# Narrower products with the low part of v, one copy on GpSimd moved, and a fixed order that ends one product later

## The chip, the cores and the metric

The kernel runs on one core of a Trainium2 chip. A core has engines with instruction streams of their own: TensorE (PE, matrix products; PEld is its loading of the stationary operand), VectorE (DVE), ScalarE (ACT), GpSimd (POOL) and SyncE (SP, which here issues the transfers between the chip's memory and the core's SBUF). Products land in PSUM and are read from there by VectorE and ScalarE. The engines run beside each other and meet through semaphores only. The metric is the device time of one execution in microseconds (us), the median of several runs.

## What is computed

One transformer block on x (2048 rows of 576): a modulated layer norm, linear attention with 32 heads of 18 columns, and a feed-forward network of 4608 hidden columns. Cut to what matters here:

```python
def reference(A_x, A_wqkv, A_wo, B_x, B_w1, B_w2, c, w_mod):
    ...
    h = _layernorm(x, axis=-1) * (1 + ca) + sa
    ...
    pq, pk = phi(q), phi(k)
    kv = jnp.einsum("bhsd,bhse->bhde", pk, v)
    z = jnp.einsum("bhsd->bhd", pk)
    num = jnp.einsum("bhqd,bhde->bhqe", pq, kv)
    den = jnp.einsum("bhqd,bhd->bhq", pq, z)[..., None] + 1e-6
    o = num / den
    ...
    x = x + ga * _A_ref(h, A_wqkv, A_wo)
    h = _layernorm(x, axis=-1) * (1 + cb) + sb
    x = x + gb * _B_ref(h, B_w1, B_w2)
    return x
```

The state sums of the title are kv and z: sums over all 2048 rows of products of pk and v.

## The kernel before

**Numbers in two parts.** TensorE works here on rounded 32-bit data (float32r). Each operand a is split into a high part, a rounded, and a low part, a minus that, rounded again; a product is then the sum of high x high, high x low and low x high. The state sums have a fourth term: pk holds its two parts side by side (`pk[t % 2]`, 128 rows x 2 x 632), and one product with the high part of v moves 128 columns of each of them, 256 in all; the product with the low part of v does the same, so low x low is summed too. v lies in five groups of seven heads (`NHC`, 126 columns, `HG`), with a column of ones that gives z.

**Stages.** The rows are worked in 16 tiles t of 128, four to a block of 512. The first stage (to about 208 us) normalises, projects to k, v and q, and sums the state: `kv_mm(t - 1)` (L581) is called once for each tile, with ten products into the three PSUM tiles kvp. The second stage (to about 370 us) takes, for each tile, pn = phi(q) / den (`q_norm`, L742), transposes it and multiplies it with the joined matrix M; the first feed-forward units run between. `attn_step` (L1192) issues, for a tile s, `prod` = phi(q) * z on GpSimd (L1195), then den and its reciprocal r on VectorE and ScalarE (L748 to L751), then on GpSimd pn = phi(q) * r (L752) and a copy of pn's last 64 columns to its padding (L754):

```python
G.tensor_mul(pn[:, :D].rearrange("p (h d) -> p h d", d=DH), a.rearrange("p (h d) -> p h d", d=DH),
             r.unsqueeze(2).to_broadcast([P, H, DH]))
G.tensor_copy(pn[:, D:], pn[:, KC * P : D])
```

`q_transpose` (L808) turns pn in five blocks of 128 columns; the fifth is columns 512 to 639 and so reads the padding. The third stage, 370 us to the end, is the main part of the feed-forward network: 17 groups of 256 hidden columns, each for two halves of the rows, 34 units in all. A unit has seven `up` products (L1323, six or eight instructions each) and 14 `down` groups (L1396, six instructions each, named ha, hb, hc, hd, he after their left operand), which run one unit later, between the next unit's up products. In the order `DOWN` the second half of a unit ends with he (m = 13), which is summed onto a PSUM bank that an hc group (m = 11) had used and VectorE had read. There are two down tiles in rotation; VectorE adds each group from PSUM to `acc` or `U` (L1404), and the next group into that bank waits for it.

**What sets the order.** A scheduler places instructions that no order is written for. For most of the program up to the end of the second unit of the main part, the order on each engine is written out: `ORDERS` is a table of places, engine by engine, and `arrange()` (L100) gives each instruction in it a dependence, without a wait, on the one ahead of it. The numbers count an engine's instructions in the order in which they were issued in the code. From the third unit on, a manual schedule over all engines holds the order of the code. `arrange()` is called between the two, when only the instructions of the first part have been made: TensorE's table ends at 2585, the last of them.

Of the kernel before, what the change touches and what calls it, by code (L numbers as in the profile page):

```python
# [16 lines left out]
P = 128  # L17
# [5 lines left out]
def kernel(ctx: ExitStack, tc, A_x, A_wqkv, A_wo, B_x, B_w1, B_w2, c, w_mod, out):  # L23
# [20 lines left out]
    HG = 7 * DH  # L44
# [7 lines left out]
    def f32(ap):  # L52
# [1 line left out]

    ORDERS = {
        "PE": """
            0-105 114 106-108 115 109-113 116-2585
        """,
        "DVE": """
            2-3 1 0 4 6-7 11-12 8 5 13-14 18 15 9 16 10 17 19-24 29 25 28 26-27 30-31 43-44 33-34 36-37 35 38 32 39  # L60
# [31 lines left out]
            382-383 386 388 390-395 397 396  # L92
        """,
        "Pool": """
            3 6 0 4-5 2 7 9 8 10-15 20 16-17 19 18 21-26 34 28 27 31 29-30 35 32 38 36 42 33 37 45 39-40 48 43-44 51
            46 41 47 55 49-50 58 52-53 61 85 56 73 57 54 59 77 60 62-63 80 64 74 65 68 75 69 78 66 72 70 79 67 76 81
            71 82-84 95 90-93 86-88 94 101 89 103 105 99-100 97 106-107 121 98 96 102 123 104 108-111 124 114 125
            113 112 115 118 116 119-120 117 122 126-128
# [8 lines left out]
    def arrange():  # L107
        for engine, text in ORDERS.items():
            traced = [i for i in nc.cur_bb.bb.instructions if i.engine == getattr(mybir.EngineType, engine)
                      and not isinstance(i, (mybir.BassTilePoolBoundary, mybir.InstTileManualSchedule))]  # L110
            before = None
            for part in text.split():
                first, *last = part.split("-")
                for i in traced[int(first) : int(last[0] if last else first) + 1]:
                    if before is not None:
                        no_wait = mybir.DependencyInfo(mybir.DependencyClass.NoSync, mybir.DependencyReason.DATA)
                        tc.add_manual_dep(i, before.name, no_wait, reason="arrange")
                    before = i
# [185 lines left out]
    def mod_ps(k):  # L304
        return kvp[k // 2][:, k % 2, :]
# [276 lines left out]
    def kv_mm(t):  # L582

        pkt, vt = pk[t % 2], vx[t % 2]
        for j in range(NHC):
            o = mod_ps(j)
            for h in range(2):
                T.matmul(  # L588
                    o, vt[:, j, h, :], pkt[:, :, j * HG : j * HG + P],
                    start=(t == 0 and h == 0 and j % 2 == 0), stop=(t == NT - 1 and h == 1),  # L590
                    skip_group_check=True,
                )
# [47 lines left out]
    with tc.manual_schedule(engines={mybir.EngineType.PE}):  # L640
        for t in range(NT):
# [35 lines left out]
            if t > 0:  # L677
                kv_mm(t - 1)
            for _ in range((0, 2, 1, 1)[t] if t < 4 else 1):
                q = next(qs)  # L680
# [9 lines left out]
    with tc.manual_schedule(engines={mybir.EngineType.PE}):  # L690
        qs = iter(range(QB, NT))
        finish_wo()
        edges_of_wo(range(NHC - 2))
        q_proj(next(qs))
        kv_mm(NT - 1)
        edges_of_wo((NHC - 2,))

# [20 lines left out]
        for j, kv in enumerate(kvp):  # L718
            n = min(2, NHC - 2 * j)
# [48 lines left out]
        for j in range(KC + 1):  # L768
            psm = ps2()
            n = wo_rows[j]  # L770
# [302 lines left out]
    def fetch(i):  # L1073
        if i < len(streamed):
            _, q, n = streamed[i]
            in_room[i] = parts = []
            left = hd[q, n].shape[1]
            for room, m in rooms0.get(i) or [(rooms[(i + 2) % 3], left)]:
                nc.sync.dma_start(f32(room[:, :m, :]), hd[q, n][:, len(parts) : len(parts) + m, :])
                parts += [room[:, a, :] for a in range(m)]  # L1080
# [427 lines left out]
    def run(tokens, units, weights):  # L1508
        for token in tokens:
            name = token.rstrip("'^")  # L1510
            if name == "ft":
                i = next(fetches)
                if i > 6:
                    fetch(i)
                continue
            late = len(token) - len(name)
            of = weights[late] if name[0] in "wgl" else units[late]
            if of:
                of.step(name)
# [3 lines left out]
    def do_unit(g, p):  # L1523
        nonlocal unit, before, behind2
        unit = Unit(g, p, ws[g])
        for q, lines in enumerate(steps(p)):
            def beside(tokens):
                run(tokens, (unit, before, behind2), (ws[g], ws.get(g + 1)))

            if unit.last and p == 1:  # L1530
                lines = [x + LAST.get((q, j), "").split() for j, x in enumerate(lines)]
            if before:
                before.down(2 * q)
            beside(lines[0])
            unit.up(ORDER[q])
            if not before and q == 1:
                rooms.append(rs.tile([P, 5, 512], F32R, name="room"))
                fetch(6)
            beside(lines[1])
            if before:  # L1540
                before.down(2 * q + 1)
            beside(lines[2])
        behind2, before = before, unit
# [3 lines left out]
    with tc.manual_schedule(engines={mybir.EngineType.PE}):  # L1547
# [3 lines left out]
        ws.update({g: Weights(g) for g in range(2, NG)})  # L1551
        for u in units[:2]:
            do_unit(*u)
    arrange()
    with tc.manual_schedule(engines=ENGINES):
        for u in units[2:]:
            do_unit(*u)
        for work, tokens in TAIL:
            unit.plain_down(work)
            run(tokens.split(), (unit, behind2), ())  # L1560
    psC.release()
    for p in (rs, ph, pf, pu, w2p, wqp, edge, wp, hTa, accp):
        p.release()
# [28 lines left out]
```

## Time and profile before

| | |
|---|---|
| median of 3 runs | 1142.06 us (1140.82 to 1143.03) |
| the profiled execution | 1139.88 us |
| its span, first to last instruction | 1138.1 us |
| granted TensorE clock, mean | 1.00 |
| ACT busy, share of the span | 47% |
| POOL busy, share of the span | 57% |
| mean transfer rate | 236 GB/s |

The profile is of one execution; the 1.8 us between its time and its span lie before the first and after the last instruction. A row of the timeline gives the start in us, the time to the end of the last of a group of equal instructions, the engine, the line of the kernel, the operation, what is written and read, the shape and the count; in brackets stands how long the engine stood idle before it and what ended that. PE's products overlap: the distance between two starts is what one costs, and a duration is longer than that. In the table by stretches a row gives, for a stretch of time, the busy time and count of PE, PEld, DVE, ACT and POOL, then the granted clock, the busy share of the transfer engines and GB/s.

### The profile page before, as it was taken

Reading aid. Unit: us, or ns where it says so; the run is one execution under the profiler, and the core shown is the slowest. Engines: PE = TensorE matmul, PEld = TensorE weight load, DVE = VectorE, ACT = ScalarE, POOL = GpSimd, SP = SyncE. Lnnn points to the kernel's source line nnn. Section 1 sums busy time; section 2 is a strip of 40 time slices with the busy share of each in tenths; the row PEclk is TensorE's granted clock in tenths of the full one; section 3 lists DMA queues with packets and bytes.
Section 4 is the critical chain, followed back from the end, with each engine's and each line's share of the span. In section 5 each row is a group of like instructions: output and inputs, shape, how many; then the busy total and the mean of one; then the engine's idle time right before and its main releaser. Section 6 shows DMA issues by size and latency. Waiting matters only on the chain.

```text
span 1138.1 us, 19287 instructions
## 1 busy us (share of the span) xinstructions
PE 1126.6 (99%) x7033; PEld 1041.0 (91%) x7033; DVE 970.6 (85%) x1543; ACT 538.8 (47%) x1112; POOL 649.4 (57%) x743
## 2 busy tenths in 40 slices
PE   8999999999999999999999999999999999999998
PEld 8999999999998889999999999999999999999998
DVE  7866743685879889999999999999999999999996
ACT  6643442547556544445444444454454444444441
POOL 2100000373715767766775777677767767776776
PEclk9999999999999999999999999999999999999999
DMA  9521100223359976977968779769678697697684
GB/s 281 198 84 33 42 7 1 71 84 115 141 194 340 350 262 252 359 270 267 346 262 330 300 257 350 273 255 363 265 284 332 265 342 285 256 344 275 258 306 156
DMA packets 58813, 269.03 MB, mean 236 GB/s; under 512 B 5724, under 2 KB 21856, under 8 KB 35680
## 3 DMA queue, kind: packets, MB, share of 16 engines
q1 hardware_dynamic: 58708, 267.80, 63.8%
q8 instruction: 56, 0.92, 0.3%
q14 instruction: 37, 0.30, 0.1%
q10 hardware_dynamic: 12, 0.00, 0.0%
HBM read 250.12 MB, written 16.78 MB: 235 GB/s over the span
## 4 chain that ended last, share of the span: by engine, by line
PE 93%; DVE 2%; DMA 1%; POOL 1%; ACT 1%; issue 0%; DVEq 0%; POOLq 0%
PE up L1323 34%; PE down L1396 32%; PE psK L226 12%; PE big L226 6%; PE big L896 2%; PE small L885 2%; PE kvp L588 2%; PE small L214 1%; DMA hT<-hd 1%; PE big L811 1%; PE psT L214 1%; PE kvp L412 1%; DMA raw<-in_w_mod_dram 1%; PE up L1426 1%; PE down L1426 1%; POOL prod L1195 0%
## 5 line engine op out<-in xcount | busy, mean ns | idle before, releaser
L1404 DVE TENSOR_TENSOR acc<-down,acc 128x576 f32<-128x576 f32 x330 | 246.2, 753 | 14.6 <-PE down L1396 5.3
L1323 PE MATMUL up<-hT,w 128*128 128x512 f32 x916 | 239.4, 390 | 0.1
L1323 PEld LDWEIGHTS up<-hT,w 128*128 128x128 f32 x916 | 164.5, 188 | 25.0 <-DMA hT<-hd 0.3
L1358 POOL TENSOR_TENSOR s<-f,f 128x256 f32<-128x256 f32 x66 | 51.6, 782 | 162.0 <-ACT f L1339 162.0
L1396 PE MATMUL down<-w,hb 128*128 128x288 f32 x792 | 120.6, 294 | 0.0
L1396 PE MATMUL down<-w,hc 128*128 128x288 f32 x792 | 120.6, 294 | 0.0
L1396 PEld LDWEIGHTS down<-w,hb 128*128 128x128 f32 x792 | 113.8, 188 | 5.1
L1396 PEld LDWEIGHTS down<-w,hc 128*128 128x128 f32 x792 | 113.7, 188 | 5.1
L121 DVE TENSOR_TENSOR w<-v,w 128x288 fp32r<-128x288 f32 (+1 forms) x170 | 114.4, 682 | 0.5 <-ACT w L1057 0.5
L1404 DVE TENSOR_TENSOR U<-down,U 128x576 f32<-128x576 f32 x132 | 99.5, 754 | 17.5 <-PE down L1396 15.6
L226 PE MATMUL psK<-w,hT 128*128 128x352 f32 (+3 forms) x506 | 106.2, 336 | 0.5 <-POOL w L317 0.5
L1323 PE MATMUL up<-room,w 128*128 128x512 f32 x348 | 91.0, 390 | 0.0
L1377 POOL TENSOR_TENSOR hc<-s,hc 128x512 fp32r<-128x512 f32 x66 | 89.4, 1354 | 0.0
L226 PEld LDWEIGHTS psK<-w,hT 128*128 128x128 f32 x506 | 82.0, 189 | 6.8 <-POOL w L317 0.7
L1339 ACT ACTIVATE f<-f 128x512 f32<-128x512 f32 x102 | 64.4, 631 | 48.9 <-DVE f L1344 26.5
L184 POOL TENSOR_TENSOR rstd<-ve,neghalf 128x4 f32<-128x4 f32 (+3 forms) x10 | 9.8, 977 | 134.5 <-DVE ve L183 134.4
L1342 DVE TENSOR_TENSOR f<-up,p 128x512 f32<-128x512 f32 x102 | 69.6, 683 | 12.8 <-PE up L1323 11.9
L1065 ACT CAST w<-v 128x288 fp32r<-128x288 f32 x85 | 36.7, 434 | 75.4 <-PE down L1396 65.9
L1362 POOL TENSOR_TENSOR f<-f,s 128x256 f32<-128x256 f32 x66 | 50.7, 769 | 36.3 <-DVE hb L1377 25.9
L1323 PEld LDWEIGHTS up<-room,w 128*128 128x128 f32 x348 | 62.5, 188 | 9.4
L1396 PE MATMUL down<-w,hd 128*128 128x288 f32 x396 | 63.0, 294 | 0.9 <-DVE acc L1404 0.9
L1396 PE MATMUL down<-w,ha 128*128 128x288 f32 x396 | 63.0, 294 | 0.0
(310 smaller groups left out, 2529.4 us busy)
## 6 DMA issues: line engine op xcount, KB each, us to landing
hT<-hd SPq DMA_DIRECT2D x66, 1280.0 KB, 5.9
hT<-hd SPq DMA_DIRECT2D x45, 1024.0 KB, 5.3
room<-hd SPq DMA_DIRECT2D x35, 1280.0 KB, 5.6
room<-hd SPq DMA_DIRECT2D x20, 1024.0 KB, 5.3
v<-in_B_w_dram SPq DMA_DIRECT2D x17, 576.0 KB, 6.7
v<-in_B_w_dram SPq DMA_DIRECT2D x17, 512.0 KB, 7.0
hd<-S SPq DMA_DIRECT2D x6, 1024.0 KB, 4.3
xt<-in_A_x_dram SPq DMA_DIRECT2D x16, 288.0 KB, 3.1
```

Source lines behind the costliest of these rows:

```text
L121: return V.tensor_sub(lo, full, f32(hi))
L214: T.transpose(ps[:, i * P : (i + 1) * P], xt[i][:, cidx * P : (cidx + 1) * P], ident)
L226: T.matmul(ps, xpart(a), wpart(b), start=n == 0, stop=n == len(XW) - 1)
L1065: A.copy(self.w2[n][:, 0], src)
L1323: T.matmul(ps, left, right, start=first and m == 0, stop=m == len(seq) - 1, skip_group_check=True)
L1339: A.activation(self.f[i, k], self.f[i, k], AF.Silu)
L1342: V.tensor_add(f, self.bank[bank[1]], self.p1)
L1358: G.tensor_add(self.s[:, 0:1], half(i, 0, 1), half(i, 1, 1))
L1362: G.tensor_sub(half(i, 1, 0), half(i, 1, 0), self.s[:, 1:2])
L1377: eng.tensor_sub(t[:, :, 1, :], src, f32(t[:, :, 0, :]))
L1396: T.matmul(ps[:, p, :HALF], self.a[i, n][:, u, p * P : (p + 1) * P], self.w.w2[n][:, v], start=n in (1, 5, 7, 6) and j == 0, stop=j == 2, ...
L1404: V.tensor_add(dst, ps[:, :, :HALF], dst)
```

## The change

```diff
     ORDERS = {
         "PE": """
-            0-105 114 106-108 115 109-113 116-2585
+            0-105 114 106-108 115 109-113 116-2586
         """,
...
         "Pool": """
-            3 6 0 4-5 2 7 9 8 10-15 20 16-17 19 18 21-26 34 28 27 31 29-30 35 32 38 36 42 33 37 45 39-40 48 43-44 51
+            3 6 0 4-5 2 7 9 8 10-15 20 16-17 19 18 21-26 34 28 27 31 29-30 35 32 38 36 33 42 37 45 39-40 48 43-44 51
...
         for j in range(NHC):
-            o = mod_ps(j)
+            o = mod_ps(j).rearrange("p (a q) -> p a q", a=2)
             for h in range(2):
+                n = 2 - h
                 T.matmul(
-                    o, vt[:, j, h, :], pkt[:, :, j * HG : j * HG + P],
+                    o[:, :n], vt[:, j, h, :], pkt[:, :n, j * HG : j * HG + P],
                     start=(t == 0 and h == 0 and j % 2 == 0), stop=(t == NT - 1 and h == 1),
...
             do_unit(*u)
-    arrange()
     with tc.manual_schedule(engines=ENGINES):
         for u in units[2:]:
             do_unit(*u)
         for work, tokens in TAIL:
             unit.plain_down(work)
             run(tokens.split(), (unit, behind2), ())
+    arrange()
```

Three things. The product with the low part of v (h = 1) takes the high part of pk alone, so low x low is no longer summed; as many products are issued. On GpSimd the copy to pn's padding with the number 33 stands ahead of a product with the number 42, and no longer behind it. And TensorE's table takes in product 2586, the first of the third unit; since that is made later, `arrange()` is called at the end.

On TensorE in the first stage, kv_mm for one tile (kvp are the PSUM tiles of the state sums, pk and vx the parts of pk and v) before:

```order
L588 MATMUL kvp_108<-pk_150,vx_152 128x256 x4
L588 MATMUL kvp_109<-pk_150,vx_152 128x256 x4
L588 MATMUL kvp_110<-pk_150,vx_152 128x256 x2
L226 MATMUL psK<-wq,hT 128x288 x56
L226 MATMUL psK<-w,hT 128x352
```

and now:

```order
L589 MATMUL kvp_108<-pk_150,vx_152 128x128
L589 MATMUL kvp_109<-pk_150,vx_152 128x256
L589 MATMUL kvp_109<-pk_150,vx_152 128x128
L589 MATMUL kvp_109<-pk_150,vx_152 128x256
L589 MATMUL kvp_109<-pk_150,vx_152 128x128
L589 MATMUL kvp_110<-pk_150,vx_152 128x256
L589 MATMUL kvp_110<-pk_150,vx_152 128x128
L226 MATMUL psK<-wq,hT 128x288 x56
```

Every second product has 128 columns; what stands around them is the same.

On GpSimd in the second stage, from the product for tile 5 on (pn_2453 is the pn of tile 3, pn_2524 that of tile 4; acc holds phi(q)), before:

```order
L1195 TENSOR_TENSOR prod_2610<-acc1_96,z_94 128x576
L752 TENSOR_TENSOR pn_2524<-acc1_96,r_2528 128x576
L1195 TENSOR_TENSOR prod_2676<-acc1_96,z_94 128x576
L754 COPY pn_2453<-pn_2453 128x64
L754 COPY pn_2524<-pn_2524 128x64
L1195 TENSOR_TENSOR prod_2768<-acc1_96,z_94 128x576
```

and now:

```order
L1196 TENSOR_TENSOR prod_2610<-acc1_96,z_94 128x576
L753 TENSOR_TENSOR pn_2524<-acc1_96,r_2528 128x576
L755 COPY pn_2453<-pn_2453 128x64
L1196 TENSOR_TENSOR prod_2676<-acc1_96,z_94 128x576
L755 COPY pn_2524<-pn_2524 128x64
L1196 TENSOR_TENSOR prod_2768<-acc1_96,z_94 128x576
```

The copy for the earlier pn is one product further ahead; the other stays behind that product.

On TensorE in the third stage, where the second unit ends and the third begins (he_4371 is the second unit's last down group, ha_4366 and hd_4387 the first two that belong to the third unit's order), before:

```order
L1396 MATMUL down<-w_4244,hc_4326 128x288 x6
L1323 MATMUL up<-hT,w 128x512 x6
L1323 MATMUL up<-hT,wtb 128x512 x2
L1396 MATMUL down<-w_4197,ha_4366 128x288 x6
L1323 MATMUL up<-hT,w 128x512 x6
L1396 MATMUL down<-w_4264,he_4371 128x288 x6
L1396 MATMUL down<-w_4206,hd_4387 128x288 x6
```

and now:

```order
L1397 MATMUL down<-w_4244,hc_4326 128x288 x6
L1324 MATMUL up<-hT,w 128x512 x6
L1324 MATMUL up<-hT,wtb 128x512 x2
L1397 MATMUL down<-w_4264,he_4371 128x288 x6
L1397 MATMUL down<-w_4197,ha_4366 128x288 x6
L1324 MATMUL up<-hT,w 128x512 x6
L1397 MATMUL down<-w_4206,hd_4387 128x288 x6
```

he stands two groups further ahead, and between it and hd there are now ha and an up product. The other engines' orders are as before, and so is that of the transfers.

## The prediction

> **What bounds the kernel now.** I read the page first: busy times and the chain of waits.
>
> ```profile
> span 1138.1 us, 19287 instructions
> ...
> PE 1126.6 (99%) x7033; PEld 1041.0 (91%) x7033; DVE 970.6 (85%) x1543; ACT 538.8 (47%) x1112; POOL 649.4 (57%) x743
> ...
> PE 93%; DVE 2%; DMA 1%; POOL 1%; ACT 1%; issue 0%; DVEq 0%; POOLq 0%
> ```
>
> The second row is busy time by engine, the third the share of the chain that ended last. TensorE (PE) works or waits for its own predecessor in 93% of the chain. So time can only come from cheaper products or from a moment in which TensorE stands still. Next I read the list of waits, kept to PE, and the table by stretches for the long main part:
>
> ```profile
> PE big L811 <- POOL pn L754: 1.0, 1, 1.0
> PE down L1396 <- DVE acc L1404: 0.9, 1, 0.9
> ```
>
> ```profile
> 500.00:700.00 200.00, 200.00 (x1194) 182.50 (x1194) 187.65 (x277) 92.37 (x201) 143.70 (x170) 1.00 0.81 305
> ```
>
> Behind 500 us TensorE has no gap in 200 us, at a granted clock of 1.00. The two waits above are single places, about 1 us each, and the two edits of order are at just these places. The third edit makes 80 of the 160 products of the state sums narrower. I take them one by one.
>
> **The narrower products.** In kv_mm each of 16 row tiles has 10 products; the 5 with the low part of v now stream 128 columns of pk and not 256. Nothing is taken away: as many products, as many weight loads. What one costs is its distance to the next start, which the timeline of PE shows:
>
> ```profile
> 79.86 1.35 PE L588 MATMUL kvp<-pk,vx 128*128 128x256 f32 x10
> 81.05 3.87 PE L226 MATMUL psK<-wq,hT 128*128 128x288 f32 x28
> 84.76 0.46 PE L226 MATMUL psK<-w,hT 128*128 128x352 f32 x2
> ```
>
> Ten products of 256 columns take 81.05 - 79.86 = 1.19 us, 119 ns each; 28 of 288 columns take 3.71 us, 132.5 ns each. So 32 columns are worth 13.5 ns here, 0.42 ns a column, and at that rate 128 columns less would save 54 ns. But narrow products early in the kernel do not go on falling:
>
> ```profile
> 8.53 0.38 PE L390 MATMUL psT<-ident,xt 128*128 128x128 f32 x2
> ...
> 9.18 0.38 PE L390 MATMUL kvp<-ident,xt 128*128 128x128 f32 x2
> ```
>
> ```profile
> 10.44 1.06 PE L371 MATMUL kvp<-sc,hT 128*128 128x64 f32 x8
> 11.33 1.56 PE L412 MATMUL kvp<-ones 128*128 128x128 f32 x12
> 12.77 1.32 PE L407 MATMUL psK<-w,hT 128*128 128x288 f32 x8
> ```
>
> Six transposes of 128 columns start within 9.18 - 8.53 = 0.65 us, 108 ns each; eight records of 64 columns (full-precision data) take 11.33 - 10.44 = 0.89 us, 111 ns each; twelve of 128 columns take 1.44 us, 120 ns each. All three have a weight load for each product, and half the columns (64 against 128) buys almost nothing: at this width the load of 128 weight columns sets the distance. No product of rounded data (float32r, which pk and vx are) narrower than 256 columns stands in this trace, so its price is bounded: 108 ns below, 120 ns (no gain) above on this reasoning. I take 111, from the row that streams least and has the same kind of load. Gain: 80 x (119 - 111) = 0.64 us, between 0 and 80 x 11 = 0.88 us. If the load were hidden by something else the gain would be larger; that is a rival below. Without the low x low part fewer terms are summed, which costs no time on any engine: the evacuation of kvp reads the same columns.
>
> **The copy on GpSimd.** q_norm writes pn in two steps, the product with r (L752) and a copy of the last 64 columns to its padding (L754). TensorE transposes five blocks of pn, and only the fifth reads the padding.
>
> ```profile
> 233.49 1.16 POOL L752 TENSOR_TENSOR pn<-acc,r 128x576 f32<-128x576 f32 x1
> 234.61 1.40 POOL L1195 TENSOR_TENSOR prod<-acc,z 128x576 f32<-128x576 f32 x1
> 235.96 0.40 POOL L754 COPY pn<-pn 128x64 f32<-128x64 f32 x2
> 236.88 1.43 POOL L1195 TENSOR_TENSOR prod<-acc,z 128x576 f32<-128x576 f32 x1 [0.52 <-DVE den L748]
> ...
> 239.50 0.24 POOL L754 COPY pn<-pn 128x64 f32<-128x64 f32 x1
> ```
>
> ```profile
> 234.67 0.60 PE L811 MATMUL big<-ident,pn 128*128 128x128 f32 x4
> 236.24 0.33 PE L811 MATMUL big<-ident,pn 128*128 128x128 f32 x1 [0.97 <-POOL pn L754]
> ...
> 243.87 0.71 PE L811 MATMUL big<-ident,pn 128*128 128x128 f32 x5
> ```
>
> Four transposes at 108 ns from 234.67 put the fifth at 235.10; it starts at 236.24, since the copy stands behind the product of 234.61. Now the copy comes at about 234.65 and, at 0.24 us (row of 239.50), ends at 234.89: 0.2 us before it is needed. Gain: 236.24 - 235.10 = 1.14 us. The price is on GpSimd: the product behind it starts 0.24 us later. Behind that product stand DVE's den and the next prod (236.88, which waits for den), and the copy of 239.50. TensorE takes that pn at 243.87, or 242.7 when it is 1.14 us earlier; 239.7 is early enough by 3 us, so the delay is covered. The copy issues no DMA and passes no queue. The lower end is 0, if GpSimd's times (rough on this page) hide a later end of the copy.
>
> **The order at the seam.** The fixed table reached to product 2585, the last of the first two units of the main part. From 2586 on another order holds, and nothing tied the two, so the first product group of the third unit (ha) and its group up had gone ahead of the last group of the second (he). The tie puts he first, then ha, then up. The timeline of PE, DVE and POOL there:
>
> ```profile
> 401.61 0.96 PE L1396 MATMUL down<-w,ha 128*128 128x288 f32 x6
> 402.40 1.53 PE L1323 MATMUL up<-hT,w 128*128 128x512 f32 x6
> 403.77 0.96 PE L1396 MATMUL down<-w,he 128*128 128x288 f32 x6
> 405.68 1.04 PE L1396 MATMUL down<-w,hd 128*128 128x288 f32 x6 [0.94 <-DVE acc L1404]
> ```
>
> ```profile
> 399.99 0.76 DVE L1404 TENSOR_TENSOR U<-down,U 128x576 f32<-128x576 f32 x1 [0.89 <-PE down L1396]
> 400.66 0.75 DVE L1404 TENSOR_TENSOR acc<-down,acc 128x576 f32<-128x576 f32 x1
> ...
> 404.77 0.76 DVE L1404 TENSOR_TENSOR acc<-down,acc 128x576 f32<-128x576 f32 x1 [2.16 <-PE down L1396]
> ```
>
> ```profile
> 391.89 0.92 POOL L1377 TENSOR_TENSOR he<-f,he 128x256 fp32r<-128x256 f32 x1
> ```
>
> he and hd use the same PSUM bank in turn: he ends, DVE adds it to acc (404.77 to 405.53), and 0.15 us later hd may start. he itself takes 402.40 - 401.61 = 0.79 us, so hd could have started at 403.77 + 0.79 = 404.56; it started 1.12 us later. In the new order he runs 401.61 to 402.40. Its data are ready (GpSimd wrote its low part by 392.8). Its bank must have been read: DVE's acc of 400.66 ends at 401.41, and with the same 0.15 us PE may go on at 401.56, 0.05 us before it gets there. Then ha and up follow and end at 404.56, and DVE, which sat idle 2.16 us before 404.77, has the sum of he done by about 403.4. hd finds its bank free. Gain 1.12 us, or 0 if DVE's read of the bank is over a microsecond later than the row says. What comes later is ha and up, by 0.79 us each; with up goes the transfer that refills its room:
>
> ```profile
> 403.97 5.29 SPq L1079 DMA_DIRECT2D hT<-hd  x2
> ```
>
> ```profile
> hT<-hd SPq DMA_DIRECT2D x2, 1280.0 KB, 5.4
> ```
>
> ```profile
> 413.73 1.53 PE L1323 MATMUL up<-hT,w 128*128 128x512 f32 x6
> ```
>
> Issued at 404.76 and landed 5.4 us later, at 410.2, it is still 2.4 us ahead of its use at 413.73 - 1.12 = 412.6. So this too is covered.
>
> **The sum.** 0.64 + 1.14 + 1.12 = 2.90 us. The profiled execution took 1139.88 us (span 1138.1 and 1.8 us around it), so it would be 1137.0; the median of the three runs is 2.2 us above it, and 1142.06 - 2.90 = **1139.2 us** is my number, 0.25% less. What a measurement of this kernel can tell from no change is about 0.2%, 2.28 us, so the forecast lies just beyond it. The three runs differ by 2.2 us among themselves, and a third of the sum going missing decides how it is read.
>
> **Rivals.** *Given back before the main part.* The first two gains (1.78 us) come before a stretch in which VectorE and the transfers are dense:
>
> ```profile
> 345.00:360.00 15.00, 14.20 (x90) 12.55 (x89) 14.33 (x20) 10.33 (x21) 8.80 (x7) 1.00 0.86 324
> ```
>
> ```profile
> 352.01 0.76 DVE L901 TENSOR_TENSOR acc<-big,acc 128x576 f32<-128x576 f32 x1 [0.21 <-PE big L896]
> ```
>
> ```profile
> 358.67 1.89 PE L885 MATMUL small<-hT,w 128*128 128x512 f32 x7 [0.55 <-DVE hT L121]
> ```
>
> DVE is busy 14.33 of 15 us and waits only 0.21 us for TensorE, while TensorE waits 0.55 us for DVE. If DVE's work there is tied to transfers (16 engines busy 0.86) that do not come earlier, TensorE waits longer and only the seam's 1.12 us is left: 1140.9 us. Against it: DVE does wait for PE at 352.01, and transfers into reused rooms are released by TensorE's last reading, so they move along. *Columns alone.* If the load hides beside two products and the 0.42 ns a column hold below 256, the products save 80 x 54 ns = 4.3 us, and the time is 1142.06 - 4.3 - 2.26 = 1135.5 us. The rows of 108 to 120 ns speak against it. The Trainium skill has this as a rule: "TensorE: Matmul & The Clock Gate", section "Back-to-back issue gap", gives a stream of loads and products 81 ns at 128 columns and 131 ns at 512. By it the products would save 80 x 38 ns = 3.0 us, an estimate from that page and the 119 ns; this trace disagrees, with 132.5 ns at 288 columns already. *Narrow products fall to the slow pace.* The one that ends on the other side: rounded products are quick in every row of 256 columns and more, and the kernel never goes below, even carrying 64 columns of v with 288 of k. If a 128-column product is streamed like full-precision data, it costs two records,
>
> ```profile
> L526 PE MATMUL psK<-ones,tmod 128*128 128x128 f32 x20 | 2.6, 275 | 0.0
> ```
>
> where 10 products in the code (five in each of two mod_col) are 20 records. At 111 ns a record that is 222 ns, +103 ns on 80 products, +8.2 us, and with the 2.26 us of the seams 1148.0 us. It decides from about 147 ns a product (119 + 2.26 us / 80). Against it: the operands' type, which splits a full-precision product into two records, is not changed. *The orders do nothing.* If both waits are set by another engine, 0.64 us is left, 1141.4 us; the rows of DVE and POOL speak against it.
>
> **Chances.** The forecast 0.68, given back 0.15, narrow at the slow pace 0.07, orders without effect 0.06, columns alone 0.04. With a spread of some 1 us in a median of three, the forecast falls below 1139.78 (faster by over 0.2%) in about four of five: 0.54, with 0.04 of columns alone and 0.02 of the second case 0.60. Slower by over 0.2% is the slow pace alone, 0.07; the rest, 0.33, is no change that can be told. The range 1136.7 to 1141.5 us takes in the forecast with its spread, the case given back and the orders without effect; outside are the slow pace, columns alone and the tails.
>
> **What would show it.** The kvp products: starts 1.15 us from first to next group, not 1.19 (1.4 or more if the slow pace holds; 0.9 if columns alone count). The fifth transpose of pn without the 0.97 us of waiting. At the seam he, ha, up, hd with no wait of hd for DVE. Both waits gone from PE's list and a span near 1135.2. The prediction is wrong if the PE wait on DVE near 358 grows by as much as was saved, if PE waits for hT in the main part, or if the narrow products' distance is over 120 ns.

## The result, and the profile after

The changed kernel took 1138.97 us (median of 13 runs, 1137.46 to 1141.10) beside 1141.44 us for the kernel before on the same chip (13 runs, 1139.66 to 1144.05). The ratio is 0.9979, with a 95% interval of 0.9971 to 0.9986: a gain of 2.47 us between the medians, 1.6 to 3.3 us by the interval. The forecast was 1139.2.

The page of the changed kernel, with the span, the busy times and the shares of the chain that ended last:

```profile
span 1136.2 us, 19286 instructions
...
PE 1125.9 (99%) x7033; PEld 1040.0 (92%) x7033; DVE 972.6 (86%) x1543; ACT 538.9 (47%) x1112; POOL 650.0 (57%) x743
...
PE 92%; DVE 3%; ACT 2%; POOL 2%; DMA 1%; issue 1%; SPq 0%; DVEq 0%; POOLq 0%; ACTq 0%
```

The span is 1.9 us shorter and TensorE is as full as it was. Its list of waits no longer has the two single waits of about 1 us (pn on GpSimd, acc at the seam). The wait for hT near 358 us, 0.6 in the list of before, is 0.7 now, and a wait for qT is new:

```profile
PE small L886 <- DVE hT L121: 0.7, 1, 0.7
...
PE big L226 <- DVE qT L121: 0.6, 1, 0.6
```

(Lines behind 587 count one more than before.) **The seam** is as forecast. TensorE there, and the sum on VectorE that frees the bank for hd:

```profile
400.49 0.98 PE L1397 MATMUL down<-w,he 128*128 128x288 f32 x6
401.31 0.99 PE L1397 MATMUL down<-w,ha 128*128 128x288 f32 x6
402.13 1.53 PE L1324 MATMUL up<-hT,w 128*128 128x512 f32 x6
403.50 0.96 PE L1397 MATMUL down<-w,hd 128*128 128x288 f32 x6
```

```profile
401.51 0.76 DVE L1405 TENSOR_TENSOR acc<-down,acc 128x576 f32<-128x576 f32 x1
```

he is summed by 402.27, and hd starts at 403.50 without a bracket. **The copy** no longer makes TensorE wait, but it gained less than a third of what was forecast. The transposes, and the products behind them:

```profile
233.74 0.71 PE L812 MATMUL big<-ident,pn 128*128 128x128 f32 x5
235.09 1.69 PE L226 MATMUL big<-w,qT 128*128 128x288 f32 x11 [0.64 <-DVE qT L121]
```

All five transposes run in one group now, the fifth 2.06 us earlier than before (236.24). But the next products start only 1.25 us earlier (236.34 before). TensorE came to the place with a lead of 0.93 us already, so 0.32 us are the copy's gain. The products behind the transposes work on another tile: on the qT of tile 2, which was transposed some 4 us earlier. They wait for its low part. VectorE at that place, and ScalarE's high part:

```profile
232.64 0.76 DVE L749 TENSOR_REDUCE den<-prod 128x32 f32<-128x576 f32 x1 [0.45 <-POOL prod L1196]
233.31 0.45 DVE L178 BATCH_NORM_STATS2 st<-acc 128x6 f32<-128x288 f32 x1
233.91 0.35 DVE L752 RECIPROCAL r<-den 128x32 f32<-128x32 f32 x1 [0.15 <-POOL pn L755]
234.18 0.76 DVE L121 TENSOR_TENSOR qT<-big,qT 128x640 fp32r<-128x640 f32 x1
```

```profile
230.89 0.67 ACT L814 CAST qT<-big 128x640 fp32r<-128x640 f32 x1
```

The high part was written by 231.56, so the low part could have been made as soon as VectorE was free. In VectorE's fixed order it stands behind den, which waits 0.45 us for GpSimd's product, and behind r. It ends at 234.94; TensorE goes on 0.15 us later. The same low part and the same products before:

```profile
235.10 0.76 DVE L121 TENSOR_TENSOR qT<-big,qT 128x640 fp32r<-128x640 f32 x1
```

```profile
236.34 1.83 PE L226 MATMUL big<-w,qT 128*128 128x288 f32 x12
```

The low part ended at 235.86 and TensorE came at 236.34: the wait for the copy had covered it.

**The narrow products** (kvp):

```profile
79.54 1.26 PE L589 MATMUL kvp<-pk,vx 128*128 128x256 f32 x10
80.64 3.93 PE L226 MATMUL psK<-wq,hT 128*128 128x288 f32 x28
84.41 0.45 PE L226 MATMUL psK<-w,hT 128*128 128x352 f32 x2
```

Ten products (the order list ahead of the prediction shows the last seven) take 80.64 - 79.54 = 1.10 us and not 1.19, but the 28 behind them take 3.77 and not 3.71, so 0.03 us is left at this tile. Over all 16 tiles, from the first kvp product to the fourth behind the group, the starts add up to 0.71 us less: 1.55 us inside the groups, of which the products right behind them pay 0.83 back.

To see where each gain went I compared the start of the same product of TensorE, by its number, with the profiled execution of before. Executions are already up to 1.7 us apart at 49.8 us, so the table counts from there. It gives the gain in us in each stretch (by the time of before), for the changed kernel and the experiments that follow; a minus is a loss.

| | to 234.7 | 234.7 to 236.3 (copy) | to 400.9 | 400.9 to 407.8 (seam) | to 897.7 | behind |
|---|---|---|---|---|---|---|
| the change | 0.83 | 0.32 | -0.13 | 1.18 | -0.77 | 0.38 |
| narrow products alone | 0.63 | -0.01 | -0.32 | 0.04 | -1.29 | 0.39 |
| copy alone | -0.17 | 0.32 | -0.36 | 0.00 | 0.00 | 0.39 |
| seam alone | 0.00 | -0.01 | -0.17 | 1.19 | 0.00 | 0.39 |
| copy and qT | 0.05 | 1.21 | -0.99 | 0.00 | -1.67 | 0.20 |
| the change and qT | 0.75 | 1.21 | -0.76 | 1.18 | 0.00 | 0.39 |
| the same and H | 0.78 | 1.20 | -0.57 | 1.19 | 0.00 | 0.38 |
| the same and hT | 0.25 | 1.21 | -0.71 | 1.18 | 0.00 | 0.39 |

The columns of the copy and of the seam repeat to 0.02 us in all executions with the same orders there. The other four need care. The last is alike nearly everywhere and belongs to the execution of before. Of the third, about 0.2 us is no effect either: "seam alone" changes nothing ahead of 400 us and loses 0.17 there. In the first, "copy alone" loses 0.17 us without a change ahead of it, and "the same and hT" loses about 0.6 us near 122 us, where TensorE waits 0.41 us for VectorE's vx, at a place that none of its edits touches. The losses of the fifth come back under "What stays open".

### The profile page after: what moved, and what is told of

Same layout as the page of the kernel before. It is cut to its first block, busy times and chain, and to the rows that moved or that the text cites. A ratio compares the mean times of both kernels' runs of the same rounds, so it can differ in the third digit from the quotient of the medians.

```text
span 1136.2 us, 19286 instructions
## 1 busy us (share of the span) xinstructions
PE 1125.9 (99%) x7033; PEld 1040.0 (92%) x7033; DVE 972.6 (86%) x1543; ACT 538.9 (47%) x1112; POOL 650.0 (57%) x743
## 4 chain that ended last, share of the span: by engine, by line
PE 92%; DVE 3%; ACT 2%; POOL 2%; DMA 1%; issue 1%; SPq 0%; DVEq 0%; POOLq 0%; ACTq 0%
PE up L1324 34%; PE down L1397 32%; PE psK L226 13%; PE big L226 4%; PE big L897 2%; PE small L886 2%; PE kvp L589 2%; DMA room<-hd 1%; PE small L214 1%; POOL prod L1196 1%; PE psT L214 1%; PE up L1427 1%; PE down L1427 1%; DMA hT<-in_w_mod_dram 0%; PE big L812 0%
## 5 line engine op out<-in xcount | busy, mean ns | idle before, releaser
L1397 PE MATMUL down<-w,he 128*128 128x288 f32 x396 | 63.0, 294 | 0.0
```

The costliest lines, as they stand in the source:

```text
L1397: T.matmul(ps[:, p, :HALF], self.a[i, n][:, u, p * P : (p + 1) * P], self.w.w2[n][:, v], start=n in (1, 5, 7, 6) and j == 0, stop=j == 2, ...
```

## The experiments

My theory after the result: the three parts are separate; the narrow products gain some 9 ns each because the load of 128 weight columns sets their distance; the copy's gain is cut by a VectorE operand that stands late in a fixed order; and what comes out of the second stage is partly given back where VectorE is dense. The main rivals: a part gives nothing at all, the narrow products gain or lose by their columns, or the gain of the copy is bound to a transfer and not to an order.

### Each part alone

The narrow products alone:

```diff
-            o = mod_ps(j)
+            o = mod_ps(j).rearrange("p (a q) -> p a q", a=2)
...
+                n = 2 - h
...
-                    o, vt[:, j, h, :], pkt[:, :, j * HG : j * HG + P],
+                    o[:, :n], vt[:, j, h, :], pkt[:, :n, j * HG : j * HG + P],
```

> The kernel before with the narrower products alone (low x low of the state sums is left out, as in the changed kernel). In the profiles of before and of the change TensorE's lead grew by 0.91 us between 49.8 and 203.5 us. Theory: this is all theirs and reaches the end, so the ten state-sum products take 1.10 us where they took 1.19, the lead is about 0.9 us at 203 us and the same 0.9 us at the end, the waits for the copy of pn (0.97 us) and at the seam (0.94 us) stay as they were, ratio to before 0.9992. Rival: what waits on GpSimd is not moved along, so the wait for the copy grows to about 1.9 us and the lead behind it is 0: ratio 1.000.

Measured: 1140.84 us, ratio 0.9993 (0.9984 to 1.0002). By the median not to be told from no change; by the trace the tiles gain 0.72 us, as in the full change. The other two waits are as they were. What the profiled execution lost, it lost at two transfers of the main part, of which this is one:

```profile
826.69 1.75 PE L1397 MATMUL down<-w,hc 128*128 128x288 f32 x12
828.87 1.43 PE L1324 MATMUL up<-hT,w 128*128 128x512 f32 x5 [0.43 <-DMA hT<-hd]
```

The copy alone:

```diff
-            ... 35 32 38 36 42 33 37 45 39-40 48 43-44 51
+            ... 35 32 38 36 33 42 37 45 39-40 48 43-44 51
```

> The kernel before with the copy on GpSimd moved alone. Theory: the wait for the copy goes, but the next products need the low part of qT, which VectorE had ready only at about 236.0 us in the profile of before, so TensorE waits for VectorE (about 0.6 us in the list of waits) and only some 0.3 us of the 1.14 us are won; ratio 0.9997. Rival, the forecast's term: no new wait and 1.14 us won, ratio 0.9990.

Measured: 1140.77 us, ratio 0.9994 (0.9985 to 1.0002). TensorE at the transposes:

```profile
234.71 0.71 PE L811 MATMUL big<-ident,pn 128*128 128x128 f32 x5
236.05 1.16 PE L226 MATMUL big<-w,qT 128*128 128x288 f32 x7 [0.64 <-DVE qT L121]
```

The interval holds both ratios that were expected, so the trace decides. The new wait is there with the same 0.64 us, without the narrow products, and the copy alone gains 0.32 us here and not 1.14. Up to 400 us this execution loses 0.36 us again, 0.2 us more than "seam alone".

The seam alone:

```diff
-            0-105 114 106-108 115 109-113 116-2585
+            0-105 114 106-108 115 109-113 116-2586
...
-    arrange()
     with tc.manual_schedule(engines=ENGINES):
...
+    arrange()
```

> The kernel before with the fixed order ending one product later, alone. Theory: he ahead of ha takes away the 0.94 us wait of hd for VectorE, TensorE's lead is 1.0 to 1.1 us at 410 us and stays to the end, ratio 0.9991. Rival: the lead is given back to transfers (a wait of PE or its weight loads for hT or room in the main part) and the end comes less than 0.4 us earlier, ratio over 0.9996.

Measured: 1139.86 us, ratio 0.9990 (0.9981 to 0.9999). This is the one part whose interval leaves out 1. It does not leave out the rival's 0.9996; that is left to the table. TensorE's waits still have the copy:

```profile
PE big L811 <- POOL pn L754: 1.0, 1, 1.0
```

The table gives 1.19 us at the seam, and none of it is lost behind. The gains of the three parts by their ratios (0.8, 0.7 and 1.1 us, each to about 1 us) add up to 2.6 us beside 2.4 for the change: nothing shows that the parts help or hinder each other.

### The operand that is late next

VectorE's low part of qT (number 297) goes ahead of den (314) in the changed kernel. By the order of the transposes it is the qT of tile 2; the expectations call it that of tile 3.

```diff
-            ... 302 307 291 314 292 315 297 323
+            ... 302 307 291 297 314 292 315 323
```

> The changed kernel with one more move: on VectorE the low part of the qT of tile 3 goes ahead of the den that waits for GpSimd's product, three places further ahead. Theory: the 0.64 us wait for qT goes, the products behind the transposes start at about 234.2 us and not at 235.09, and some 0.85 us more are won: ratio 0.9971 to before, where the change has 0.9979; den of that tile comes 0.2 us later and has 3 us of cover. Rival: another wait takes its place once more (for GpSimd's next pn, or for VectorE's den and r that are now later), and the time is that of the changed kernel, ratio 0.9979.

Measured: 1138.13 us, ratio 0.9974 (0.9964 to 0.9984). TensorE at the transposes and 25 us later:

```profile
234.45 0.71 PE L812 MATMUL big<-ident,pn 128*128 128x128 f32 x5
234.92 2.36 PE L226 MATMUL big<-w,qT 128*128 128x288 f32 x16
...
260.96 0.66 PE L214 MATMUL small<-ident,xn 128*128 128x128 f32 x4 [0.94 <-ACT H L199]
```

The wait for qT is gone, and the place gains 1.21 us: about the 1.14 that was forecast for the copy. So the order was the cause, and no transfer. It is 0.89 us more than in the change, but 0.63 us of that are lost again by 400 us, and the interval holds the ratios of the theory and of the rival. 25 us later a wait for ScalarE's H has grown to 0.94 us. It was 0.43 us before:

```profile
261.86 0.66 PE L214 MATMUL small<-ident,xn 128*128 128x128 f32 x4 [0.43 <-ACT H L199]
```

ScalarE there in the new run:

```profile
259.92 0.32 ACT L750 ACTIVATE den<-den,eps 128x32 f32<-128x32 f32 x1 [0.58 <-DVE den L749]
260.14 1.43 ACT L199 ACTIVATE H<-small,col_b 128x512 f32<-128x512 f32 x2
```

H stands behind den in ScalarE's order, and den waits 0.58 us for VectorE, as long as it did before; now TensorE comes early enough to feel more of it. It is the same pattern on the next engine.

The two edits of order without the narrow products and the seam:

```diff
-            ... 302 307 291 314 292 315 297 323
+            ... 302 307 291 297 314 292 315 323
...
-            ... 35 32 38 36 42 33 37 45 39-40 48 43-44 51
+            ... 35 32 38 36 33 42 37 45 39-40 48 43-44 51
```

> The kernel before with the copy moved on GpSimd and the qT of tile 3 moved ahead on VectorE; the products and the seam as before. Theory: the wait for the copy and the wait for qT lie in series behind one another, 0.3 and 0.85 us, so the pair wins at 236 us the 1.1 us that the forecast gave the copy alone; then ScalarE's first reading of a transposed block near 261 us (0.43 us of waiting in the kernel before) does not come as much earlier and takes back 0.4 to 0.5 us; net lead 0.6 to 0.7 us behind 262 us. Rival: nothing is taken back and the lead at 360 us is 1.1 us.

Measured: 1140.83 us, ratio 0.9993 (0.9984 to 1.0003), no better than the copy alone. TensorE's waits:

```profile
PE small L214 <- ACT H L199: 0.9, 1, 0.9
...
PE small L885 <- DVE hT L121: 0.9, 1, 0.9
PE up L1323 <- DMA hT<-hd: 0.6, 1, 0.6
```

The 1.21 us are won, and 0.99 are given back by 400 us: 0.5 at H, as the theory had it, and most of the rest at the wait for hT near 358 us. About 0.2 us of that "seam alone" loses as well. This execution then lost 1.67 us at two transfers of the main part.

Next, H (number 241) ahead of den (270) on ScalarE, on top of the change and qT:

```diff
-            ... 240 237-238 270 241 243 246
+            ... 240 237-238 241 270 243 246
```

> The changed kernel with qT first on VectorE, and on ScalarE the first reading of a transposed block near 260 us ahead of the den that waits for VectorE. Theory: with qT first TensorE waits 0.94 us for that reading; it can now start at about 259.6 and not at 260.14 us, so the wait falls to about 0.4 us and 0.5 us more stay won: ratio 0.9969 to 0.9970 to before. Rival: den is late now and GpSimd's next pn with it, and the wait moves there: no gain on the kernel with qT first, 0.9974.

Measured: 1138.41 us, ratio 0.9971 (0.9960 to 0.9983). TensorE at the two places:

```profile
260.25 0.66 PE L214 MATMUL small<-ident,xn 128*128 128x128 f32 x4 [0.43 <-ACT H L199]
...
357.58 1.90 PE L886 MATMUL small<-hT,w 128*128 128x512 f32 x7 [0.94 <-DVE hT L121]
```

The wait for H is back at 0.43 us, and the wait for hT, 0.55 in the kernel before, is 0.94. Of the 0.5 us that should have stayed, 0.19 is left at 400 us (0.57 lost and not 0.76): the gain went to the next wait, though not to the one for pn that the rival named.

Last, that hT (number 461) ahead of the long product on S (472) on VectorE, on top of it all:

```diff
-            ... 477 484 462 483 472 465 461 478 473 485
+            ... 477 484 462 483 461 472 465 478 473 485
```

> The complete kernel with three places of the fixed orders besides the change: VectorE's low part of qT ahead of den, ScalarE's H ahead of its neighbour (both as in the run before), and VectorE's low part of hT, which TensorE waited 0.94 us for at 357.58, ahead of the product on S of 1.76 us and one low part of w. Theory (series work on an engine's fixed order takes each gain back at the next operand that TensorE needs): the wait near 357.6 goes, TensorE keeps 0.9 us more until 367, span about 1134.7, ratio about 0.9963. Rival (VectorE's stretch is tied to its own work or to transfers, so the wait only moves): another wait of 0.5 to 0.9 us appears between 358 and 375, or in the main part for a transfer of hT, span about 1135.5, ratio 0.997.

Measured: 1138.11 us, ratio 0.9976 (0.9967 to 0.9985). The rival holds in kind, with a new wait of 0.43 us. TensorE and VectorE:

```profile
355.38 3.00 PE L886 MATMUL small<-hT,w 128*128 128x512 f32 x12
...
360.31 0.53 PE L897 MATMUL big<-w,hs 128*128 128x288 f32 x2
361.28 6.47 PE L897 MATMUL big<-w,hs 128*128 128x288 f32 x46 [0.43 <-DVE hs L121]
```

```profile
358.94 0.75 DVE L902 TENSOR_TENSOR acc<-big,acc 128x576 f32<-128x576 f32 x1
359.60 0.68 DVE L1140 TENSOR_TENSOR H<-H,S 128x512 f32<-128x512 f32 x1
360.20 0.42 DVE L121 TENSOR_TENSOR w<-raw,w 128x256 fp32r<-128x256 f32 x1
360.54 0.69 DVE L121 TENSOR_TENSOR hs<-sl,hs 128x512 fp32r<-128x512 f32 x1
```

The wait for hT is gone and TensorE is 1.1 us further ahead at 357. Four us later it waits for hs, whose low part VectorE writes as the next of a row of operations without a gap between them. By 376 us the lead is back to about that of the run before (0.98 and 1.06 us at 400 us).

The timeline of VectorE ahead of that row shows what the move cost:

```profile
354.68 1.76 DVE L121 TENSOR_TENSOR hT<-S,hT 128x512 fp32r<-128x512 f32 x1
356.36 0.68 DVE L1138 TENSOR_TENSOR S<-S 128x512 f32<-128x512 f32 x1
...
357.73 0.69 DVE L121 TENSOR_TENSOR S<-S 128x512 fp32r<-128x512 f32 x1 [0.35 <-ACT S L1084]
```

ScalarE's S needs the product on S, which now comes later, so VectorE waits 0.35 us for ScalarE, and the row behind starts 0.28 us later than in the run before. One operand was moved ahead and made another late. That VectorE's work here allows no better order is not shown. Nor did the 1.76 us go along with the product on S: the low part of hT took them when it stood at that place, and the product, moved behind it, 0.68. In both runs GpSimd works on its own H beside it (354.60 to 355.88 us here); whether that stretches the operation is open. The three versions with more orders lie at 1138.1 to 1138.4 us; their intervals overlap with that of the change, so none is shown to be better than it.

### What sets the distance of narrow products

The product with the low part of v moves 64 columns and not 128, with all else as changed:

```diff
-                n = 2 - h
+                n, w = 2 - h, P // (1 + h)
...
-                    o[:, :n], vt[:, j, h, :], pkt[:, :n, j * HG : j * HG + P],
+                    o[:, :n, :w], vt[:, j, h, :], pkt[:, :n, j * HG : j * HG + w],
```

> The changed kernel with 64 columns and not 128 in the products with the low part of v (half of low x high is left out). Theory that the weight load sets the distance: the ten products of a tile take as long as in the changed kernel, 1.10 us, within 0.03. Theory that the columns set it (0.42 ns each): 5 x 27 ns less, 0.96 us for a tile and 2.1 us less in all.

Measured in one execution: 1139.98 us, 1.0 us above the median of the change. Against the kernel before it lost 1.02 us between 236 and 400 us and 0.85 in the main part, so the time says little here and the groups say more:

```profile
171.97 1.24 PE L589 MATMUL kvp<-pk,vx 128*128 128x256 f32 x10
173.04 0.54 PE L226 MATMUL psK<-w,hT 128*128 128x352 f32 x2
173.42 0.46 PE L226 MATMUL psK<-v,hT 128*128 128x352 f32 x2
```

The group takes 1.07 us (1.10 with 128 columns), and the product behind it more; to the fourth product behind the group the 16 tiles gain 0.73 us. Half the columns are worth 0.02 us in all. The trace also has the start of each load of weights (PEld). Inside a group the loads start 116 ns apart on the average, with 64 columns as with 128; before, with wide products alone, it was 120.

Three products of 128 columns for each group of heads, in place of one of 256 and one of 128. All four terms but low x low are there, as in the change:

```diff
-            for h in range(2):
-                n = 2 - h
+            for n, (h, m) in enumerate(((0, 0), (0, 1), (1, 0))):
...
-                    o[:, :n], vt[:, j, h, :], pkt[:, :n, j * HG : j * HG + P],
+                    o[:, m], vt[:, j, h, :], pkt[:, m, j * HG : j * HG + P],
...
```

> The changed kernel with the product with the high part of v cut into two of 128 columns, so 15 products of 128 columns for a tile and no wide one. Theory that the weight load sets the distance: 15 x 107 to 111 ns, 1.6 to 1.67 us for a tile, about 0.5 us more than the changed kernel and some 8 us more in all. Theory that the columns set it: 15 x about 62 ns, 0.93 us for a tile, and some 2.7 us less in all.

Measured in one execution: 1148.8 us, span 1146.9. The run differs from the change in one more thing than was expected. It issues 80 more products on TensorE, so the numbers of the fixed order, which count products, no longer reach the seam: there the old order is back, ha, up, he, hd, with the wait of hd for VectorE (0.94 us). Of the 10.7 us that the span is longer than that of the change, 1.2 us come from there and 8.3 from the groups. In the trace:

```profile
176.99 1.78 PE L588 MATMUL kvp<-pk,vx 128*128 128x128 f32 x15
178.60 0.51 PE L226 MATMUL psK<-w,hT 128*128 128x352 f32 x2
178.95 0.32 PE L226 MATMUL psK<-v,hT 128*128 128x352 f32 x1
```

Behind the first product of a group the distance depends on what ran before it: 55 to 62 ns in six tiles, 141 to 273 in ten. The others are followed after 107 to 117 ns, 111 as a rule, and the first product of 288 columns behind a group pays 182 to 189 ns and not 132. From the group's first to the second group of products behind it the tile takes 178.95 - 176.99 = 1.96 us, beside 173.42 - 171.97 = 1.45 us in the run before: 0.51 us for five products more, 102 ns each, though fewer columns are moved than in the kernel before. Against the change, to the fourth product behind the group, it is 104 ns each over all 16 tiles. The loads start 112 ns apart on the average. So a rounded product of 128 columns with a load of its own costs about 111 ns here, and that is not set by the columns that it moves. All loads in these runs have 128 columns, so that it is the load's own time, and not another fixed cost of a load and its product, is not shown by a run. The Trainium skill, "TensorE: Matmul & The Clock Gate", section "LDWEIGHTS (loading the stationary operand)", has the load's time as its columns over 1.2 in ns, 107 for 128: the 111 ns of this trace agree with that. The 81 ns that the Trainium skill has for a stream of 128 columns ("TensorE: Matmul & The Clock Gate", section "Back-to-back issue gap") do not hold here, with 111 ns measured.

## Why the prediction was right, and where a step failed

**The narrow products** were right in mechanism, and the size close: 0.64 us forecast, between 0 and 0.88; 0.71 and 0.72 measured. The 111 ns, chosen from the row of 64 columns, are what the run with three products showed. What the prediction did not see is how the gain comes: the next start is 56 to 66 ns behind a narrow product and 165 to 176 behind a wide one (the group's first aside), and the first product of 288 columns behind the group pays 183 to 187 ns and not 132. The sign that was given, 1.15 us from first to next group, read 1.10, since a part is paid behind the group. A pair of the two takes 231 ns on the average, where two wide ones take 240: 9 ns for each of 80 pairs make up the gain. That a load sets the distance fits all runs, but no run changed a load.

**The columns alone and the slow pace** both fall with the same two runs: 64 columns gain nothing over 128, and 111 ns is neither the 65 ns (119 - 54) of the one nor the 222 ns of the other.

**The copy on GpSimd** is the step that failed. "Gain: 236.24 - 235.10 = 1.14 us" took the fifth transpose as the end of the matter, and the list of what comes later followed only GpSimd's queue (den, the next prod, the pn of 243.87). It did not ask what the products right behind the transposes need. They need the low part of the qT of the tile before, which stood in VectorE's order behind den and r and had been covered by the wait that was taken away. With that operand moved up, the place gains 1.21 us; without, 0.32. The lower bound of 0 held, but its reason (rough times on GpSimd) was the wrong one.

**The seam** was right by its own steps: 1.12 forecast, 1.18 and 1.19 measured, no wait of hd, and the delay of ha and up covered.

**Given back before the main part** did not decide, but was no empty rival. It named VectorE's dense stretch near 358, and in the four runs with qT ahead 0.57 to 0.99 us is given back between the transposes and 400 us, the most of it there or at H. In the change itself the loss there is 0.13 us, no more than "seam alone" has; in "copy alone" and "narrow products alone" it is 0.36 and 0.32, too little more to tell. The sign that was named, a wait near 358 us that grows by as much as was saved, did not show: it grew from 0.55 to 0.70 us.

**The sum.** The measured terms, 0.71 + 0.32 + 1.18 = 2.21 us, stand against 2.90 forecast and 2.47 us between the medians, whose interval of 1.6 to 3.3 us holds both sums. That the median came so near the forecast is therefore partly luck: the forecast started from 1142.06 us, the median of three runs, where 13 gave 1141.44, and 2.90 us less than that would have been 1138.5. The terms tell more. The stated spans (near 1135.2; 1136.2 came) say the same.

**What stays open.** In some profiled executions (the change, the narrow products alone, copy and qT) TensorE loses 0.3 to 0.9 us each near 513 and 828 us, in two of the three at marked waits for a transfer of hT or its room; the run with 64 columns loses 0.8 us near 513 alone, and the others lose nothing there. These losses follow no part of the change, and I did not find what decides them.

## What to carry to other kernels

When a stall is taken away, list what the instructions right behind it need and when each of those is ready, on every engine; the operand that was second-latest sets the gain. An operand whose operation stands in a fixed order behind one that waits for another engine came next at two places here, on VectorE (qT) and on ScalarE (H). Moving it can be worth little: counted to 400 us it was 0.26 and 0.19 us, no more than what alike executions differ by, and nothing at a third place (hT), where the move made another operand late. Where an order counts instructions, an edit that issues more of them moves its end. With a load of weights for each product, cut products, not columns, once narrower ones no longer come closer together (111 ns here).

## What the hardware showed that I had not expected

- Wide and narrow products in turn are not spaced by their own widths: behind a product of 64 columns the next starts 28 to 37 ns later, behind one of 128 columns 56 to 66 ns, and the wide one pays the rest (194 to 205 and 165 to 176 ns). A single distance says little there; the pair does, with 231 ns on the average in both.
- From 256 columns down to 128 in a stream of loads and products the cost falls from about 120 ns to 111, while 288 columns cost 132. With 64 in place of 128, tried in turn with wide ones, it falls no further.
- The profiled executions of kernels that are alike up to 400 us differ by 0.2 us near one wait (0.55 us in before, 0.7 in "seam alone"), so a single trace cannot carry a claim of that size there.
